# Order of the operand loads, sub-chunk size and engine of small copies at the start of a linear-attention and two-MLP kernel

## The chip, the cores and the metric

One core of a Trainium2 chip runs the whole program. The metric is device time in microseconds (us). Three timed runs of the kernel before gave 1028.97 us (median), 1026.72 us (lowest) and 1031.26 us (highest). The engines are named as the profile names them: PE (matrix products; PEld is its weight load), DVE (vector), ACT (scalar), POOL (GpSimd), SP (the queue that issues most transfers).

## The reference

Three layers in a row, all in float32. The first is a linear attention with a decay and a bonus for the present token, for 4 sequences of 768 tokens, 8 heads of 48 values:

```python
for t in range(S):
    cur = einsum('bhd,bhe->bhde', u[None] * k[t], v[t])
    y[t] = einsum('bhd,bhde->bhe', r[t], state + cur)
    state = w[t][..., None] * state + einsum('bhd,bhe->bhde', k[t], v[t])
x = y.reshape(3072, 384)
x = ((x @ w_a) * (x @ w_b)) @ w_out            # 384 -> 1536 -> 384
h = x @ w_in                                   # 384 -> 2048
out = (max(h, 0) + alpha * min(h, 0)) @ w_out2 # 2048 -> 384
```

## The kernel before, in words

**Units.** The attention is cut into 12 units: 128 tokens of two of the four sequences, all heads. A unit's work is written in `unit(u, pr)` from line 336. It needs its operands twice: transposed (tile `T`, r, k and w of 112 partitions by 1024 values each, 1.376 MB, `ld_t`, line 378) and natural (tile `N`, three parts of 128 by 768 values, 0.393 MB each, `ld_n`, line 382), and its values (`V`, 0.393 MB, `ld_v`, line 395), which also go straight from memory into four places of the tile `Z` (`ld_z`, line 400, four transfers).

**What a unit computes.** `natural(d, p)` (line 440) makes on DVE the terms of tokens that are d apart within a sub-chunk of C tokens, C from the list `SUBS` (4 for unit 0, 8 for unit 1): a product into `e`, a sum over it (line 486), and an update of k. The result `A` is written to memory (`mb`, line 511) and read back by eight transfers of 16 KB to the diagonal blocks of `M` (`place`, line 517). Beyond C, `level(h, bs, p)` (line 545) makes the terms of two neighbouring strips of h tokens on PE (`psl`, line 567), and `extract` copies them to `M` on ACT (line 585; for unit 1 half of them on DVE, line 583). Between the levels `tree(h, p)` (line 520) scales r and k in place on DVE (a 112x1024 product and a short one for each of six h). Then r is copied to `M` (`rcopy`, line 597), k is transposed (`ktrans`), `dstate` and `state` carry the state, and `yout` (line 698) makes the rows of y for the products in `psx`, which ACT and DVE split into a high and a low part (`x`).

**Blocks.** Two units make a block of 512 tokens. `mlp1` (line 781) runs the first MLP of a block in 12 steps: 9 products into `pa`, 9 into `pb`, 9 into `acc`, each with a weight tile of its own: 36 weight tiles in all, for all six blocks. `mlp2` (line 902) does the second MLP for six chunks of tokens with 32 more weight tiles.

**Weights.** They come as 64-bit words of 384 KB a tile. `load_w` (line 270) issues the load from POOL (line 290); where a tile lies more than `WL` = 6 behind, POOL first copies one element of the finished tile six before it (`tick`, line 289), which is how the load is held back. The fourth tile waits for a zeroed tile of the first unit (line 286). Then ACT makes three steps over the tile (`sign` L295, `expo` L307, `low` L301), DVE joins them (L310), ACT writes the high part (L316) and DVE the low part. The tile in between, `ws`, has three buffers.

**The order of the work.** `Tasks` (line 35) is a planner in the program itself. Each step has an engine, a duration, an urgency (lower is earlier), and the names it reads and writes. `run()` (line 94) walks the steps through a model of the engines and of one transfer queue (0.33 MB per us and 2.2 us), and emits them in the order of the model; each engine then works strictly in that order. While the first products are not there, `filler()` (line 138) puts products of the 128x128 identity with itself (`warm`, line 988) into PE's order, from 4.5 us of the model on. The loads of units 0 and 1 have urgencies near -260 to -215 (lines 407 to 424): N of unit 0, `un`, the identity, T of unit 0, N of unit 1, T of unit 1; the values of both only after the diagonal blocks of unit 0 (`diags`, line 409). The loads of unit 2 wait for the diagonal blocks of unit 1.

## Time and profile before

| What | Value |
|---|---|
| median of three runs | 1028.97 us |
| profiled execution: span from its first to its last instruction | 1026.6 us |
| PE, PEld busy | 984.9 us, 846.2 us |
| DVE busy | 743.5 us |
| ACT, POOL busy | 419.1 us, 91.3 us |
| mean granted clock of PE | 0.990 |
| first products of the first MLP | at 78.93 us |
| first products of the second MLP | at 614.34 us |

The profiled execution has a span of 1026.6 us; the page gives no other time for it, so the time around the span is taken as what the median of the timed runs has more, 2.4 us. All times within the span count from its first instruction. Busy times of PE overlap a little, since matmuls are pipelined; an engine that is idle matters only where another that sets the end waits for it.

### The profile page before, as it was taken

What the parts mean: (1) busy time and instruction counts of PE and PEld (TensorE: products, weight loads), DVE (VectorE), ACT (ScalarE), POOL (GpSimd) and SP (SyncE); (2) the same over time, 40 slices, a digit from 0 to 9 for tenths busy, and PEclk for the clock granted to TensorE, in tenths of its full rate; (3) what the DMA queues carried; (4) which work ended last, traced back from release to release, by engine and by line L of the source; (5) the groups of instructions that cost most, each with busy time, mean ns of one, the idle gap of its engine ahead of it and who ended that gap; (6) DMA issues with size and microseconds to landing.
All of it is one profiled execution on the core that took longest, in us unless ns stands there. A gap on an engine that the chain in (4) does not pass through costs nothing.

```text
span 1026.6 us, 22621 instructions
## 1 busy us (share of the span) xinstructions
PE 984.9 (96%) x9616; PEld 846.2 (82%) x9616; DVE 743.5 (72%) x1241; ACT 419.1 (41%) x866; POOL 91.3 (9%) x173
## 2 busy tenths in 40 slices
PE   5879989999999999999999999999999999999998
PEld 5778767887788878778888888999998999998988
DVE  7869898979989999898944667455555554555544
ACT  2477988433332353534347994121221211211111
POOL 3033230100100010001003341000000000000000
PEclk9889999999999999999999999999999999999999
DMA  9584573052341434315115551010010100000000
GB/s 273 112 238 138 161 232 111 32 142 61 113 122 22 126 85 106 111 33 171 19 42 185 169 184 63 1 31 31 18 45 1 31 31 1 1 32 1 31 1 31
DMA packets 75092, 85.70 MB, mean 83 GB/s; under 512 B 55216, under 2 KB 64560, under 8 KB 72368
## 3 DMA queue, kind: packets, MB, share of 16 engines
q1 hardware_dynamic: 67824, 52.81, 19.0%
q0 software_dynamic: 7168, 31.46, 9.3%
q8 instruction: 75, 1.23, 0.5%
q14 instruction: 25, 0.20, 0.1%
HBM read 73.24 MB, written 11.01 MB: 82 GB/s over the span
## 4 chain that ended last, share of the span: by engine, by line
PE 61%; DVE 18%; ACT 10%; DMA 5%; issue 4%; SPq 1%; ACTq 0%; DVEq 0%
PE acd L769 20%; PE hp L769 19%; PE pa L769 6%; PE acc L769 5%; PE pb L769 5%; DVE T L257 4%; DVE e L257 4%; DVE A L486 3%; DMA T<-in_rkw_t_dram 2%; PE warm L988 2%; ACT ws L295 2%; PE psl L567 2%; ACT ws L301 2%; DMA n<-in_rkw_n_dram 2%; DVE a L257 2%
## 5 line engine op out<-in xcount | busy, mean ns | idle before, releaser
L769 PE MATMUL acd<-w,g 128*128 128x384 f32 x1152 | 216.5, 336 | 0.0
L769 PE MATMUL hp<-x,w 128*128 128x512 f32 x864 | 214.9, 393 | 0.7 <-DVE g L927 0.7
L769 PEld LDWEIGHTS acd<-w,g 128*128 128x128 f32 x1152 | 203.8, 188 | 7.9
L769 PEld LDWEIGHTS hp<-x,w 128*128 128x128 f32 x864 | 161.0, 188 | 30.9 <-DVE g L927 1.1
L932 ACT CAST g<-g 128x512 fp32r<-128x512 f32 x96 | 59.6, 621 | 299.6 <-PE acd L769 262.2
L257 DVE TENSOR_TENSOR g<-g,g 128x512 fp32r<-128x512 f32 x96 | 66.1, 689 | 152.3 <-ACT g L932 151.9
L769 PE MATMUL acc<-g,w 128*128 128x512 f32 x648 | 174.5, 398 | 0.0
L769 PE MATMUL pa<-x,w 128*128 128x512 f32 x648 | 162.2, 394 | 4.0 <-DVE w L257 1.8
L769 PE MATMUL pb<-x,w 128*128 128x512 f32 x648 | 160.0, 391 | 0.2 <-DVE a L257 0.2
L769 PEld LDWEIGHTS pa<-x,w 128*128 128x128 f32 x648 | 121.4, 189 | 31.3 <-DVE w L257 2.5
L769 PEld LDWEIGHTS pb<-x,w 128*128 128x128 f32 x648 | 121.4, 188 | 26.5 <-DVE a L257 0.8
L769 PEld LDWEIGHTS acc<-g,w 128*128 128x128 f32 x648 | 118.1, 188 | 24.5 <-DVE g L257 0.2
L257 DVE TENSOR_TENSOR T<-T 112x1024 f32<-112x1024 f32 (+3 forms) x144 | 116.0, 808 | 17.2 <-DMA T<-in_rkw_t_dram 13.2
L831 ACT CAST g<-a 128x512 fp32r<-128x512 f32 x72 | 44.5, 618 | 117.0 <-DVE a L257 115.0
L923 DVE TENSOR_SCALAR g<-hp,al 128x512 f32<-128x512 f32 x96 | 72.0, 750 | 21.1 <-PE hp L769 18.4
L486 DVE TENSOR_REDUCE A<-e 128x16 f32<-128x768 f32 (+15 forms) x148 | 85.8, 579 | 1.9
L927 DVE SCALAR_TENSOR_TENSOR g<-hp,g 128x512 f32<-128x512 f32 x96 | 66.3, 690 | 2.9
L820 ACT COPY a<-pa 128x512 f32<-128x512 f32 x72 | 42.0, 583 | 55.2 <-PE pa L769 54.9
L257 DVE TENSOR_TENSOR a<-a,pb 128x512 f32<-128x512 f32 x72 | 49.1, 682 | 17.5 <-PE pb L769 16.1
L567 PEld LDWEIGHTS psl<-T 48*16 48x16 f32 (+3 forms) x3072 | 34.0, 98 | 27.6 <-issue 14.1
L257 DVE TENSOR_TENSOR g<-a,g 128x512 fp32r<-128x512 f32 x72 | 49.4, 686 | 7.4 <-ACT g L831 7.2
L567 PE MATMUL psl<-T 48*16 48x16 f32 (+3 forms) x3072 | 37.4, 183 | 17.6 <-DVE T L257 10.5
(68 smaller groups left out, 885.5 us busy)
## 6 DMA issues: line engine op xcount, KB each, us to landing
raw<-in_wt_dram POOLq DMA_DIRECT2D x68, 384.0 KB, 4.1
T<-in_rkw_t_dram SPq DMA_DIRECT2D x12, 1344.0 KB, 8.5
N<-in_rkw_n_dram SPq DMA_DIRECT2D x10, 1152.0 KB, 6.7
x2d<-x POOLq DMA_DIRECT2D x36, 128.0 KB, 2.1
x2r<-x2d SPq DMA_DIRECT2D x36, 128.0 KB, 2.2
out_dram<-o SPq DMA_DIRECT2D x24, 192.0 KB, 1.9
V<-in_v_s_dram SPq DMA_DIRECT2D x11, 384.0 KB, 5.6
Z<-in_v_s_dram SPq DMA_DIRECT2D x44, 96.0 KB, 3.0
```

The lines of the kernel that those rows point to most:

```text
L257: nc.vector.tensor_tensor(out=out, in0=a, in1=b, op=op)
L295: nc.scalar.activation(out=c["s"].bitcast(F16).rearrange("p (n b) -> p n b", b=2)[:, :, 1], in_=c["raw"][:, :, 1].bitcast(F32), func=ACTF. ...
L301: nc.scalar.activation(out=c["s"].bitcast(U16).rearrange("p (n b) -> p n b", b=2)[:, :, 0], in_=c["raw"][:, :, 0], func=ACTF.Copy, scale=7 ...
L486: nc.vector.tensor_reduce(out=v[:, :, d:d + (n - 1) * (SUB + 1) + 1:SUB + 1], in_=part(st["e"], 0, n), axis=AX.X, op=ALU.add)
L567: nc.tensor.matmul(out=st["ps"][o0:o0 + ms, cc, q, zc * i:zc * i + zc], lhsT=t[b0:b0 + 48, 1, q0 + q, t0:t0 + ms], rhs=r[b0:b0 + 48, q0 + ...
L769: nc.tensor.matmul(out=out, lhsT=lhsT, rhs=rhs, start=start, stop=stop)
L820: nc.scalar.copy(c["a", f], c["pa"])
L831: nc.scalar.copy(c["g", f][:, 0], c["a", f])
L923: nc.vector.tensor_scalar(out=st["m", f], in0=st["h", f], scalar1=0.0, scalar2=al[:, f:f + 1], op0=ALU.min, op1=ALU.mult)
L927: nc.vector.scalar_tensor_tensor(out=st["m", f], in0=st["h", f], scalar=0.0, in1=st["m", f], op0=ALU.max, op1=ALU.add)
L932: nc.scalar.copy(st["g", f][:, 0], st["m", f])
L988: nc.tensor.matmul(out=warm["ps"][:, 0:128], lhsT=idt, rhs=idt, start=True, stop=True)
```

## The change

`SUBS[1]` goes from 8 to 4, so unit 1 has four distances on DVE and one more level (h = 4) on PE. The transposed operands come in three transfers each (k, r, w) and are the first that SP issues, for unit 0; then N of unit 0, T and N of unit 1, the identity, the values. The values no longer wait for the diagonal blocks, nor do the loads of unit 2. The four transfers into `Z` of each unit become four POOL copies from `V`. The first six weight loads wait for the last natural operand of unit 1 (POOL reads one element of it). `expo` moves from ACT to POOL; `ws` has two buffers in place of three; slots of the weight pool may be taken in any order. For units 0 and 1 the state and y are made in two halves of 64 tokens (`dstate` and `yout`), `rcopy` copies only the second half, DVE takes fewer of unit 1's copies from `psl` and one more of `kn`. `warm` multiplies a tile of ones that DVE sets, from 1.5 us of the model on. The urgencies of the first block and of the weights change. The cut-down diff (comments that were dropped, and changes of names only, are left out):

```diff
-SUBS = [4, 8, 4, 8, 16, 16, 16, 16, 16, 16, 16, 16]
+SUBS = [4, 4, 4, 8, 16, 16, 16, 16, 16, 16, 16, 16]
...
-    ANY = ("ws", "psacc")
+    ANY = ("ws", "psacc", "w")
...
+    ones = const.tile([128, 128], F32, name="ones")
...
-    for tag, n in (("w", NW), ("ws", 3), ("x2", 2), ...
+    for tag, n in (("w", NW), ("ws", 2), ("x2", 2), ...
...
-        gate = len(prev) == int(4)
-        if gate:
-            after = list(after) + ["m1/d3"]
+        gate = not prev
+        prev.append(nm)
+        if len(prev) <= WL and nm[1] in "abo":
+            after = list(after) + ["N1in"]
...
-                nc.gpsimd.tensor_copy(tick, first_m[1][0:1, 0, 0, 0:1])
+                nc.gpsimd.tensor_copy(tick, cur["N", 1][2][0:1, 0, 0:1])
...
-            nc.scalar.activation(out=h, in_=h, func=ACTF.Copy, scale=2.0 ** -112)
+            nc.gpsimd.tensor_single_scalar(out=h, in_=h, scalar=2.0 ** -112, op=ALU.mult)
...
-        add("ACT", act(384), pr, expo, r=[raw], w=[raw + "/h"])
+        add("Pool", 1.2, pr, expo, r=[raw + "/h"], w=[raw + "/h"])
...
-        def ld_z():
-            for cc in range(2):
-                for hd in range(2):
-                    nc.sync.dma_start(
-                        out=zv(cc, hd)[64 * hd:64 * hd + 64], in_=v_s[u, 64 * cc:64 * cc + 64, hd])
+        def cp_z(cc, hd):
+            nc.gpsimd.tensor_copy(zv(cc, hd)[64 * hd:64 * hd + 64], cur["V", u][64 * cc:64 * cc + 64, hd])
...
-        p0 = pr(0) - 30 if u > 1 else -220 + 2 * u
+        p0 = pr(0) - 30 if u > 1 else -260 + 4 * u
...
-        after_diag = diags[1] if u == 2 else []
...
+        for i, y in enumerate("krw"):
+            add("SP", 0.45, p0 + i, lambda y=y: ld_t(y), r=[f"{T}/new"], ..., nbytes=112 * 4096)
+        for i, y in enumerate("krw"):
+            add("SP", 0.3, p0 + (1.1 + 0.1 * i if u > 1 else 3 + 0.1 * i), lambda y=y: ld_n(y), ..., nbytes=128 * 3072)
...
-            r = diags[0] if u < 2 else []
-            add("SP", 0.6, p1, ld_v, r=r, w=[V], ...)
-            add("SP", 2.4, p1, ld_z, r=r, ...)
+            add("SP", 0.6, p1, ld_v, w=[V], ...)
+            for cc in range(2):
+                for hd in range(2):
+                    add("Pool", 0.9, p1 + 30, lambda cc=cc, hd=hd: cp_z(cc, hd), r=[V], w=[zn(cc, hd, "V")])
...
-                    if both and hd:
+                    if both and hd and h >= 16:
                         nc.vector.tensor_copy(dst, src)
...
+            if early:
+                dst, src = dst[:, :, 1], src[:, :, 1]
...
+            if early:
+                for i in range(nd):
+                    add("PE", 0.7, p + i, lambda i=i: run((i,)), r=[kn + "/0", kn + "/1", V], ...)
+                return
...
+            if early:
+                add("PE", 0.8, p - 1, lambda: mms((0,)), ..., r=[x for x in mr if not x.endswith("R")] + ...)
+                add("PE", 0.8, p, lambda: mms((1,)), w=[ps], work=1024, r=mr + zr[1])
...
-            natural(d, pr(-0.1))
+            natural(d, pr(-0.1) if not early else pr(0.1))
...
-    K.fill = [lambda: fill(), 0.22, 4.5, 400.0]
+    K.fill = [lambda: fill(), 0.22, 1.5, 400.0]
...
-        nc.tensor.matmul(out=warm["ps"][:, 0:128], lhsT=idt, rhs=idt, start=True, stop=True)
+        nc.tensor.matmul(out=warm["ps"][:, 0:128], lhsT=ones, rhs=ones, start=True, stop=True)
...
-        start = [52]
+        start = [40]
...
-            start.append(start[-1] + max(..., 100 if j == 0 else 0))
+            start.append(start[-1] + max(..., 95 if j == 0 else 0))
...
+                if u < 2:
+                    names += unit(u, lambda x, u=u: -120 + 40 * x + 5 * u)
+                    continue
```

## Rows read from the trace of the kernel before

**Rows 1.** Busy time by stage: window, length, PE, PEld, DVE, ACT, POOL, PEclk, DMA share, GB/s.
```profile
0.00:78.90 78.90, 57.27 (x1416) 54.13 (x1417) 59.36 (x105) 39.97 (x99) 19.67 (x32) 0.89 0.75 208
78.90:185.80 106.90, 98.82 (x1514) 79.43 (x1512) 98.11 (x171) 86.96 (x197) 25.58 (x43) 1.00 0.52 150
185.80:274.00 88.20, 86.01 (x1095) 69.89 (x1094) 80.27 (x142) 33.28 (x61) 3.93 (x8) 1.00 0.33 91
274.00:559.00 285.00, 279.62 (x3311) 228.45 (x3310) 248.17 (x434) 121.18 (x254) 17.55 (x37) 0.99 0.33 91
559.00:623.00 64.00, 63.35 (x280) 52.12 (x279) 42.97 (x78) 62.51 (x133) 21.35 (x51) 1.00 0.49 163
623.00:1026.60 403.60, 399.84 (x2010) 362.20 (x2008) 214.60 (x315) 75.22 (x127) 3.22 (x6) 1.00 0.07 22
```

**Rows 2.** The chain that ended last, its first 80 us: start, us, what.
```profile
4.01 17.46 DMA n<-in_rkw_n_dram
...
30.99 4.85 PE warm L988 x21
...
59.79 2.22 issue
```

**Rows 3.** Busy time by short windows, columns as in Rows 1.
```profile
3.00:4.00 1.00, 0.00 (x0) 0.00 (x0) 0.84 (x2) 0.00 (x0) 1.00 (x1) 1.00 1.04 390
...
24.00:26.00 2.00, 0.00 (x0) 0.00 (x0) 2.00 (x3) 0.00 (x0) 0.00 (x0) 0.89 0.98 228
```

**Rows 4.** Instructions in order of time: DVE, SP, ACT and PE to 186 us.
```profile
30.17 2.36 DVE L257 TENSOR_TENSOR T<-T 112x1024 f32<-112x1024 f32 x2 [1.64 <-DMA T<-in_rkw_t_dram]
...
50.54 0.25 DVE L486 TENSOR_REDUCE A<-e 128x2 f32<-128x96 f32 x1
...
50.81 0.33 SPq L511 DMA_DIRECT2D mb<-A  x1
...
56.16 5.26 SPq L518 DMA_DIRECT2D M<-mb  x8
...
66.77 0.82 ACT L585 COPY M<-psl 8x128 f32<-8x128 f32 x4
...
78.93 2.32 PE L769 MATMUL pa<-x,w 128*128 128x512 f32 x9
...
185.80 2.20 PE L769 MATMUL pa<-x,w 128*128 128x512 f32 x9
```

**Rows 5.** Groups of DVE and ACT, 0 to 78.9 us: xcount | busy us, mean ns | idle before, releaser.
```profile
L257 DVE TENSOR_TENSOR T<-T 112x1024 f32<-112x1024 f32 x13 | 15.8, 1223 | 8.4 <-DMA T<-in_rkw_t_dram 4.9 <-PE psl L567 3.5
...
L257 DVE TENSOR_TENSOR e<-n,n 128x480 f32<-128x480 f32 x1 | 0.7, 653 | 0.0
...
L316 ACT CAST w<-ws 128x384 fp32r<-128x384 f32 x10 | 5.0, 503 | 0.0
...
L585 ACT COPY m<-psl 4x64 f32<-4x64 f32 x4 | 0.8, 204 | 11.4 <-DMA m<-mb 11.3
```

**Rows 6.** Groups of ACT and POOL, 78.9 to 185.8 us, columns as in Rows 5.
```profile
L307 ACT ACTIVATE raw<-raw 128x384 f32<-128x384 f32 x25 | 14.0, 560 | 0.3
...
L289 POOL COPY tick<-w 1x1 f32<-1x1 f32 x21 | 15.0, 715 | 54.6 <-ACT w L316 54.6
L290 POOL DMA_DIRECT2D raw<-in_wt_dram x21 | 11.3, 538 | 1.9 <-issue 0.7 <-DVE e L257 0.6 <-DVE g L257 0.3
```

**Rows 7.** Instructions of POOL and DVE in order of time, 96 to 101 us.
```profile
96.01 3.44 POOL L289 COPY tick<-w 1x1 f32<-1x1 f32 x1 [12.09 <-ACT w L316]
99.93 0.17 POOL L289 COPY tick<-w 1x1 f32<-1x1 f32 x1
...
97.13 1.22 DVE L257 TENSOR_TENSOR T<-T 112x1024 f32<-112x1024 f32 x1
99.33 0.68 DVE L257 TENSOR_TENSOR a<-a,pb 128x512 f32<-128x512 f32 x1
```

**Rows 8.** POOL's groups over the whole span: a zeroing of 2048 values a partition.
```profile
L977 POOL MEMSET Z<- 128x2048 f32 x1 | 1.8, 1805 | 0.3 <-POOLq L1133 0.3
```

More of the change, by code (lines that the diff above doesn't have):

```diff
@@ L354, in bank @@
         def bank(lev):
-            if u < len(BLOCKS[0]) and lev:
+            if early and u:
                 return "acc", "psacc"
@@ L553, in level @@
             tag, pool = bank(True)
-            nf = NF[h] if u < len(BLOCKS[0]) and K.fill else 0
             def mms():
@@ L617, in cp @@
                     cur["kn", u] = new_kn().rearrange("p (q d) -> p q d", d=112)
-                nc.scalar.copy(cur["kn", u][:, 4 * g:4 * g + 4], st[g])
+                if both and g:
+                    nc.vector.tensor_copy(cur["kn", u][:, 4 * g:4 * g + 4], st[g])
+                else:
+                    nc.scalar.copy(cur["kn", u][:, 4 * g:4 * g + 4], st[g])
             add("PE", 0.4, p, tr, r=[f"{T}/k.{g}", "idt"], w=[ps], alloc=(pool, ps), work=392)
-            add("ACT", act(448, True), p, cp, r=[ps], w=[f"{kn}/{g}"], alloc=("kn", kn) if g == 0 else None)
+            add("DVE" if both and g else "ACT", act(448, True), p, cp, r=[ps], w=[f"{kn}/{g}"], alloc=("kn", kn) if g == 0 else None)
         def dstate(p):
@@ L626, in dstate, with run @@
             tag, pool = bank(False)
-            def run():
+            def run(ccs=tuple(range(nd))):
                 k, v = cur["kn", u], cur["V", u]
-                pss = [pp.tile([128, 8, D], F32, tag=tag, name=f"psd{i}", bufs=3) for i in range(nd)]
-                cur["ds", u] = pss
+                pss = cur.setdefault(("ds", u), {})
+                for i in ccs:
+                    pss[i] = pp.tile([128, 8, D], F32, tag=tag, name=f"psd{i}", bufs=3)
                 for q in range(8):
                     for hd in range(2):
-                        for cc in range(nd):
+                        for cc in ccs:
                             hh = hd ^ cc
@@ L998, in rwkv_then_moe_kernel @@
             add("HOST", 0, -310, lambda: None, w=[n + "/x"], alloc=("w", n))
-        add("DVE", 0.5, -201, lambda: zeros(nc.vector, [cur["A", 0]] + A16), w=["A16", "A0/x"])
-        add("DVE", 1.0, -200, lambda: zeros(nc.vector, St), w=[f"St{i}.{b}" for i in range(2) for b in range(2)])
+        add("Pool", 0.5, -205, lambda: zeros(nc.gpsimd, [cur["A", 0]]), w=["A0/x"])
+        add("DVE", 0.1, -400, lambda: nc.vector.memset(ones, 1.0), w=["ones"])
+        add("DVE", 0.3, -199, lambda: zeros(nc.vector, A16), w=["A16"])
+        add("DVE", 1.0, -199, lambda: zeros(nc.vector, St), w=[f"St{i}.{b}" for i in range(2) for b in range(2)])
         def first():
@@ L1053, in weights @@
                     next(gens[i - n], None)
-        weights((load_w((nm, f), wt1[f, i], start[0] + (start[1] - start[0]) / F1 * f - wlead + i)
-                 for f in range(F1) for i, nm in enumerate("abo")), WL - 1)
+        d = (start[1] - start[0]) / F1
+        w1 = [("a", f, 0) if i == 0 else ("b", f, 1) if i == 1 else ("o", f, 2) for f in range(F1) for i in range(3)]
+        weights((load_w(f"w{nm}{f}", wt1[f, i], start[0] + d * (f + 0.3 * i) - wlead - (25 if f < 2 else 0))
+                 for nm, f, i in w1), WL - 1)
         for j in range(NB):
@@ L1068, in rwkv_then_moe_kernel @@
         s2 = start[NB]
-        w2 = [("ip"[i], f) for f in range(F2) for i in range(2)]
-        weights((load_w((nm, f), wt2[f, "ip".index(nm)], start[NB - 1] + 4 + 1.8 * i, ["p2"])
-                 for i, (nm, f) in enumerate(w2)), min(4, WL - 1))
+        weights((load_w(f"w{'ip'[i]}{f}", wt2[f, i], start[NB - 1] + 4 + 3.6 * f + 1.8 * i, ["p2"])
+                 for f in range(F2) for i in range(2)), WL - 1)
         d = 63.0
```

155 lines of the change are left out of this document (73 added, 82 removed).

## The prediction

> **What bounds the kernel now.** I read the busy time by stage first. From 78.9 us on PE is busy 98.82 of 106.90, 86.01 of 88.20, 279.62 of 285.00, 63.35 of 64.00 and 399.84 of 403.60 us [rows 1]: 927.6 of 947.7. The reader is to see that behind the first product of the first MLP PE sets the end nearly alone; 20 us of idle time are all that a better order can win there, and 8.1 of them lie in block 0 (78.9 to 185.8 us). DVE has 98.11 us of work in the 106.90 of block 0 and is 89% busy from 185.8 to 559 us (328.5 of 373.2) [rows 1]: it follows PE closely, so an earlier PE is of use only where DVE comes along.
>
> So the question is why the first product starts at 78.93 us [rows 4]. In the chain of waits its head is a transfer, N of unit 1, for 17.46 us; then PE's filler products and short stops called "issue" [rows 2]. In order of time, DVE's first product on T of unit 1 waits until 30.17 us, the last sum of unit 1's natural terms starts at 50.54, `mb` is issued at 50.81, its way back into M takes SP from 56.16 to 61.42, ACT's copies that need it begin at 66.77, and the product follows at 78.93 [rows 4]. From `mb` to the product are 28.1 us. PE was not short of time there: much of its 57 us of work is filler.
>
> **The loads.** Before the operands of unit 1 six weight tiles of 0.393 MB went out, 2.36 MB in all, and T of unit 1 was the last. Alone on the queues T moved at 228 GB/s; N moved at 390 [rows 3]. Now T of unit 0 comes first, then N, then T and N of unit 1. With a start of the flow at 2.4 us (an estimate, from the busy window at 3 us in rows 3): 1.376 / 0.228 = 6.0, so T at 8.4; 1.18 / 0.39 = 3.0, so N at 11.4; T of unit 1 at 17.4 and its N at 20.4 us. All 5.11 MB at the one or the other rate bound the last landing at 15.5 and 24.8. SP issues six transfers for T in place of two and is past all of its loads in under 10 us; the values, now ahead of the diagonal blocks on SP, are 0.8 MB behind N. The weights pay: POOL stands at its first tick until N of unit 1 is there, and behind it stand six weight loads and eight copies into Z, for which `sign` on ACT and `yout` wait. They land between about 22 and 29 us; the first product needs two of them by 50 or so, so this wait is hidden; without that cover it costs what R2 prices.
>
> **DVE up to `mb`.** Eight distances are 9696 values a partition in products, sums and updates; four are 5184. At 653 ns for 480 [rows 5] a value costs 1.36 ns: 13.2 against 7.1 us, 6 us saved. From 8.4 us DVE has the natural terms of unit 0 (7.1) and three levels of its tree (1.22 [rows 5] and about 0.5 for the short part, 5.2), which is 20.7 us, when N of unit 1 is there; then unit 1's terms (7.1) and two levels (3.4): `mb` goes out at about 31 us in place of 50.8. Nothing on DVE before 8.4 us is missed.
>
> **From `mb` to the first product.** The 28.1 us [rows 4] are the way out and back and the copies behind it. The new level costs ACT 16 copies of 0.204 us [rows 5], 3.3 us, and ACT takes over what DVE copied of h = 8, about 1 us. Eight transfers into Z fall away on SP, `rcopy` is halved, state and y come in halves, and half of a `kn` copy goes to DVE: some 3 us. The write of `mb` no longer meets the weights, which are in by 29 us. Less queueing at ACT (the ACT copies began 5.3 us behind SP's last issue) may give 3 us more, and the rest of unit 0's tree, seven products of 1.22 us, still has to run on DVE beside it. I take 25 us, from 20 to 31. The first product then starts at 31 + 25 = 56 us, 23 earlier, with ends of 46 and 66.
>
> **Block 0.** `expo` leaves ACT: 25 tiles of 0.560 us, 14.0 us of the 86.96 that ACT works there [rows 1, 6]. But 10 tiles were finished before the first product [rows 5]; with loads from 22 us on and the two units packed I count about 5. So five more tiles fall into block 0, 5.5 us for DVE, and its 98.1 us become 103.6.
> A POOL operation of 384 values has no row. Between a zeroing of 2048 in 1805 ns [rows 8], scaled to 0.34 us, and the 0.560 us that ACT took for the step, I take 0.34, as the zeroing ran on POOL itself. What it costs DVE: the one-element copy at 96.01 lasted 3.44 us, to 99.45, while DVE ran products of two operands in SBUF, and ended just behind the start of one (99.33) that takes its second operand from PSUM; the copy at 99.93 took 0.17 [rows 7]. So POOL's reads wait for such gaps, and what DVE loses lies between nothing and the whole of 0.56 for each of 31 `expo` and 8 copies into Z: 0 to 22 us. I take half of 0.34 each, 7 us, nearer to nothing because in the row it is POOL that waits. DVE then has 110.6 us; some 2 us of it can slip, as the last part of block 0 holds terms of unit 4. Block 0 goes from 106.9 to 109 us, +2; ends: 98.8 (all idle time of PE gone) and 129.
> The Trainium skill (SBUF — State Buffer, "Who interferes with whom") states that a DVE instruction with two SBUF inputs and a GpSimd instruction that reads SBUF exclude each other for the whole instruction, and that whichever is issued first blocks the other. The trace agrees for POOL (3.44 against 0.17 us); that DVE is held as well no row here shows, and by the rule the 7 us would be 13 at 0.34 each.
>
> **Later.** 32 copies into Z fall into blocks 1 to 4, 0 to 18 us for DVE by the same bounds, beside 44.7 us of idle time of DVE [rows 1]; I take 2 us, 0 to 8. In the second MLP `expo` costs nothing: from 559 to 623 us ACT is busy 62.51 of 64 us, yet PE 63.35 [rows 1], so PE's products cover it; were they gone, 32 tiles of 0.34 us on POOL would show. Two `ws` buffers instead of three are covered as long as a tile leaves them fast (R2). The tile of ones lets filler run 4 us sooner, on no chain.
>
> **The sum** on the profiled execution: 1026.6 - 23 + 2 + 2 = 1007.6 us. The median of the runs lies 2.4 above the span: 1010 us, or 19 below 1028.97. Since PE's own work behind the first product stays, the gain at the start should reach the end.
>
> **Rivals.** *R1, POOL's queue holds the weights.* For each tile POOL has a tick of 0.715, an issue of 0.538 [rows 6] and now `expo` of 0.34 plus a wait like the tick's (0.715 - 0.17 = 0.55): 2.14 us; 31 tiles are 66 us, within block 0. If its two reads wait 1.4 us each it is 3.9 us a tile, block 0 becomes 121 us, and the time 1010 + 12 = 1022. For it: the 3.44 us [rows 7], and POOL is strictly in order, so `expo` stands behind ticks that wait for ACT. Against: the mean tick. *R2, slower: two buffers of `ws` with a step on POOL between.* A tile is now held through ACT, POOL, ACT, DVE, ACT and DVE. If only two tiles are ready at the first product, 34 go through two buffers; at 8 us each they need 136 us. Block 0 grows by 27 over my 109 and the time is 1037. It decides from 7.8 us a tile on. For it: DVE and ACT are both near full in block 0 [rows 1]; against: the bare work of a tile is about 4 us, and planned urgencies put tiles ahead. The same mechanism with the weights later still only lengthens it. *R3, more is won.* The first product at 50, the idle time of PE in block 0 gone (-8.1) and nothing lost later: 1026.6 - 29 - 8 + 2.4 = 992. For it: ACT loses 14 us of work just where its steps fill the stretch. *R4, the change does not do what it says:* PE's order is that of the planner's model, filler included; if that order keeps PE as late as now, the time is about 1027 to 1029. Against it: filler is put in only where the model has nothing else.
>
> **How the numbers follow.** Forecast 0.55, with a range of its own of 1002 to 1019; R1 0.16, R2 0.12, R3 0.13, R4 0.04. About 0.5% (5 us) is what a measurement of this kernel can tell from no change, so faster means below 1023.8. Faster: 0.55 + 0.13 + 0.07 of R1 = 0.75; same: 0.09 of R1 + 0.04 = 0.13; slower: 0.12. The range of 994 to 1030 leaves out R2 and a part of R3; its ends come from a first product at 46 with block 0 as before or shorter, and from block 0 at 129 us.
>
> **What would show it.** The first product (`pa`) near 56 us; T of unit 1 on DVE by about 18 us; `mb` of unit 1 at about 31; the first product of block 1 near 56 + 109 = 165 us in place of 185.80 [rows 4]; PE's idle time behind it no larger than now. Wrong it would be if `pa` starts late because ACT or SP, not DVE, holds unit 1; if block 0 lasts over 120 us with waits of `pa`, `pb` on weights (R1: POOL waits for DVE; R2: `sign` waits for a `ws`); or if DVE's two-operand products become longer beside POOL and later blocks wait for `x`.

## The result, and the profile after

The changed kernel takes 1042.65 us (median of four runs, 1042.48 to 1044.37), the kernel before 1027.85 us on the same chip (1024.07 to 1031.26). The ratio is 1.0148, 95% interval 1.0119 to 1.0176: 1.5% slower, outside the predicted range of 994 to 1030 us, where a time of 1010 us had been forecast. The profiled execution has a span of 1040.9 us against 1026.6.

Busy time by stage of the kernel after, cut where the first product of a block (`pa`) starts; columns as in [rows 1]:

```profile
0.00:78.40 78.40, 66.86 (x1625) 63.84 (x1626) 60.43 (x97) 28.21 (x91) 28.14 (x34) 0.93 0.62 186
78.40:193.30 114.90, 99.90 (x1487) 78.63 (x1486) 98.57 (x160) 83.54 (x183) 82.23 (x97) 0.93 0.46 139
193.30:282.40 89.10, 88.09 (x1106) 72.31 (x1105) 81.72 (x143) 33.12 (x61) 10.14 (x14) 1.00 0.29 83
282.40:559.60 277.20, 269.59 (x3262) 220.02 (x3261) 241.23 (x422) 111.06 (x234) 29.93 (x42) 0.99 0.25 73
559.60:631.00 71.40, 71.40 (x317) 59.12 (x316) 42.21 (x73) 51.26 (x97) 49.70 (x82) 1.00 0.53 167
631.00:1040.90 409.90, 406.45 (x2038) 367.35 (x2036) 225.70 (x335) 88.80 (x153) 17.62 (x23) 1.00 0.08 27
```

Before it can be compared, a bound of [rows 1] has to be put right. PE's timeline of the kernel before shows three starts of nine `pa` products there; a block has 108 of them, and the 109th is the one at 179.00. So 185.80 us is step 1 of block 1, not its start:

```profile
172.86 2.22 PE L769 MATMUL pa<-x,w 128*128 128x512 f32 x9
...
179.00 2.20 PE L769 MATMUL pa<-x,w 128*128 128x512 f32 x9
...
185.80 2.20 PE L769 MATMUL pa<-x,w 128*128 128x512 f32 x9
```

The busy time of the kernel before, block 0 between its true bounds:

```profile
78.90:179.00 100.10, 92.02 (x1484) 73.80 (x1482) 91.31 (x161) 85.16 (x193) 25.30 (x42) 1.00 0.55 160
```

The reader is to see three things. The first product comes at 78.4 us where it came at 78.9: the start won nothing. Block 0 takes 114.9 in place of 100.1 us, with PE idle for 15.0 in place of 8.1 us and busy for 7.9 us longer at a mean granted clock of 0.93 in place of 1.00. And from block 1's first product to the end it is 847.6 us in both kernels: blocks 1 to 5 take 2.4 us longer in the kernel after, and the second MLP 2.4 us less. So on balance the whole loss, 14.3 us of span, arises in block 0.

What PE waited for in block 0 of the kernel after:

```profile
PE acc L777 <- ACT g L839: 4.5, 3, 3.4
PE psl L557 <- DVE T L258: 4.5, 2, 3.2
PE psx L714 <- issue: 3.7, 1, 3.7
PE pa L777 <- DVE w L258: 1.3, 1, 1.3
```

Each line gives the us in total, the times and the longest. PE waits for a finished tile (`w`) for only 1.5 us (0.2 of it in a smaller group); it waits for ACT and DVE, which also prepare the tiles, and once for "issue", a stop for which the profile names no cause (more on these under No. 10). The three long waits (3.2, 3.7 and 3.4 us, ending at 91.6, 125.5 and 185.4 us) are 10.3 of the 15.0 us of idle time, and during or right behind each of them the granted clock fell to 0.50, the lower of its two levels, 1.2 GHz (90.3 to 97.1, 124.4 to 131.3 and 185.9 to 189.3 us). The 7.9 us of longer busy time go with these three spells: in block 0 the kernel before had no wait over 2.1 us and a clock of 1.00.

The start of the kernel after in order of time (timelines of DVE, SP, ACT, POOL and PE, put together; start, duration, and idle time before with its releaser):

```profile
8.74 1.23 DVE L258 TENSOR_TENSOR T<-T 112x1024 f32<-112x1024 f32 x1 [2.34 <-DMA T<-in_rkw_t_dram]
20.82 1.62 POOL L293 COPY tick<-n 1x1 f32<-1x1 f32 x1 [16.29 <-DMA n<-in_rkw_n_dram]
30.87 1.23 DVE L258 TENSOR_TENSOR T<-T 112x1024 f32<-112x1024 f32 x1 [3.09 <-PE psl L557]
43.52 0.34 SPq L504 DMA_DIRECT2D mb<-A  x1
47.14 1.11 ACT L323 CAST w<-ws 128x384 fp32r<-128x384 f32 x2 [15.88 <-DVE ws L317]
48.15 6.05 ACT L575 COPY m<-psl 4x64 f32<-4x64 f32 x29
54.11 3.90 ACT L575 COPY M<-psl 4x64 f32<-4x64 f32 x24
60.65 0.96 DVE L258 TENSOR_TENSOR e<-N,un 128x768 f32<-128x768 f32 x1 [4.74 <-DMA N<-in_rkw_n_dram]
67.31 1.12 ACT L302 ACTIVATE ws<-raw 128x384 f16<-128x384 f32 x2
```

The transfers land as predicted (8.74 and 20.82 us), and `mb` of unit 1 goes out 7.3 us sooner than before (43.52 against 50.81, [rows 4]), though not at 31. But the 28.1 us from `mb` to the first product became 34.9, and the start was level again. ACT made the first steps over two tiles by 31.3 us and then stood 15.88 us at the first `hi`, as DVE came to the `join` in front of it only at 46.55 us, behind the terms of unit 1. The copies of both units followed, and ACT began the next tile (`sign`) at 67.31 us.

**All kernels, read in the same way.** "Ready" counts weight tiles whose `hi` began before the first product; "36th" is the start of the last `hi` of the first MLP's tiles; then the first products of block 1 and of the second MLP. "Median" is that of the timed runs, in us. The other times come from one profiled execution of each kernel. That of No. 14 is the slowest of its 12 runs (1033.31 us) and that of No. 15 the fastest of its 9 (1021.64 us), so 2 or 3 us between two rows can be chance. The ratio is to the kernel before, timed on the same chip, where its median was 1027.85 us for the kernel after and 1029.72 to 1031.45 for the others; a forecast in us is to be read with that in mind.

| No. | Kernel | 1st product | Ready | 36th | Block 1 | MLP 2 | Median | Ratio to before, 95% |
|---|---|---|---|---|---|---|---|---|
| | before | 78.9 | 10 | 175.1 | 179.0 | 614.3 | 1027.85 | 1 |
| | after | 78.4 | 4 | 191.9 | 193.3 | 631.0 | 1042.65 | 1.0148 [1.0119, 1.0176] |
| 1 | after, no `expo` | 87.5 | 5 | 183.3 | 183.9 | 626.4 | 1039.56 | 1.0077 [1.0052, 1.0101] |
| 2 | after, `expo` on ACT | 86.9 | 4 | 195.8 | 196.2 | 633.3 | 1049.44 | 1.0173 [1.0143, 1.0204] |
| 3 | after, three `ws` | 79.5 | 6 | 181.5 | 183.4 | 626.2 | 1040.46 | 1.0082 [1.0056, 1.0108] |
| 4 | after, Z by transfer | 86.5 | 6 | 189.9 | 191.6 | 630.7 | 1044.87 | 1.0124 [1.0090, 1.0157] |
| 5 | after, 30 tiles | 79.8 | 4 | 173.0 (30th) | 179.0 | 629.7 | 1041.81 | 1.0097 [1.0060, 1.0134] |
| 6 | after, no filler | 73.7 | 4 | 185.8 | 187.1 | 625.4 | 1036.94 | 1.0058 [1.0034, 1.0081] |
| 7 | after, unit 2 held back | 77.7 | 4 | 189.9 | 192.2 | 631.5 | 1043.24 | 1.0105 [1.0064, 1.0146] |
| 8 | after, natural first | 81.9 | 5 | 187.3 | 189.6 | 629.6 | 1039.71 | 1.0082 [1.0055, 1.0109] |
| 9 | before, no filler | 75.0 | 9 | 174.4 | 177.2 | 613.7 | 1027.39 | 0.9978 [0.9960, 0.9995] |
| 10 | before, sub-chunks of 4 | 88.2 | 7 | 179.2 | 191.1 | 624.0 | 1039.34 | 1.0106 [1.0071, 1.0141] |
| 11 | after, weights not held | 86.1 | 6 | 189.3 | 189.5 | 627.6 | 1040.18 | 1.0109 [1.0082, 1.0137] |
| 12 | after, three `ws`, no filler | 74.2 | 4 | 176.8 | 181.7 | 625.3 | 1036.94 | 1.0074 [1.0048, 1.0099] |
| 13 | after, sub-chunks of 8 | 87.7 | 7 | 189.8 | 191.0 | 630.8 | 1042.05 | 1.0115 [1.0088, 1.0141] |
| 14 | before, weights held | 80.1 | 10 | 179.4 | 185.0 | 619.3 | 1030.74 | 1.0001 [0.9981, 1.0021] |
| 15 | before, weights held, no filler | 72.5 | 9 | 172.2 | 176.3 | 607.7 | 1022.47 | 0.9946 [0.9922, 0.9969] |
| 16 | after, path of a tile as before | 80.4 | 5 | 180.1 | 183.1 | 629.7 | 1039.95 | 1.0089 [1.0058, 1.0121] |
| 17 | before, path of a tile as after | 79.0 | 8 | 186.6 | 188.4 | 624.5 | 1039.55 | 1.0094 [1.0058, 1.0130] |
| 18 | after, weights' steps late, no filler | 74.9 | 2 | 190.7 | 189.2 | 627.9 | 1040.01 | 1.0086 [1.0052, 1.0120] |

Two limits of block 0 can be read from the table. Block 1 starts 0 to 6 us behind the 36th tile in all kernels but No. 10 (11.9 us) and No. 18 (its product came 1.5 us ahead). And it starts 96 us or more behind the first product: 96.4 to 109.3 us where that comes at 86 us or later (Nos. 1, 2, 4, 10, 11 and 13), 114.9 in the kernel after. The first of these is an order in time and shows no cause yet; Nos. 5, 16 and 17 try it.

### The profile page after: what moved, and what is told of

Read it like the earlier page. It is cut to its first block, busy times and chain, and to the rows that moved or that the text cites. A ratio compares the mean times of both kernels' runs of the same rounds, so it can differ in the third digit from the quotient of the medians.

```text
span 1040.9 us, 23170 instructions
## 1 busy us (share of the span) xinstructions
PE 1002.3 (96%) x9826; PEld 861.3 (83%) x9826; DVE 749.9 (72%) x1226; ACT 396.0 (38%) x817; POOL 217.8 (21%) x290
## 4 chain that ended last, share of the span: by engine, by line
PE 66%; DVE 21%; issue 4%; DMA 3%; ACT 3%; POOL 2%; SPq 1%; DVEq 0%; POOLq 0%; ACTq 0%
PE acd L777 19%; PE hp L777 19%; PE acc L777 7%; PE pa L777 7%; PE pb L777 6%; DVE T L258 5%; DVE e L258 4%; DVE A L479 3%; PE warm L995 3%; DMA T<-in_rkw_t_dram 2%; DVE a L258 2%; PE psl L557 2%; DVE N L258 2%; DVE g L258 2%; DMA N<-in_rkw_n_dram 2%
## 5 line engine op out<-in xcount | busy, mean ns | idle before, releaser
L777 PE MATMUL acc<-g,w 128*128 128x512 f32 x648 | 177.8, 404 | 4.5 <-ACT g L839 4.5
L940 ACT CAST g<-g 128x512 fp32r<-128x512 f32 x96 | 59.6, 621 | 295.8 <-PE acd L777 255.2
L777 PE MATMUL pb<-x,w 128*128 128x512 f32 x648 | 163.0, 396 | 0.8 <-DVE a L258 0.5
L777 PEld LDWEIGHTS acc<-g,w 128*128 128x128 f32 x648 | 122.0, 193 | 31.0 <-ACT g L839 5.3
L258 DVE TENSOR_TENSOR T<-T 112x1024 f32<-112x1024 f32 (+4 forms) x144 | 121.9, 846 | 24.5 <-DMA T<-in_rkw_t_dram 16.2
L314 POOL TENSOR_SCALAR raw<-raw 128x384 f32<-128x384 f32 x68 | 90.6, 1339 | 82.6 <-ACT ws L302 79.7
L404 POOL COPY Z<-V 64x384 f32<-64x384 f32 x40 | 35.6, 891 | 246.5 <-PE psx L714 238.5
L479 DVE TENSOR_REDUCE A<-e 128x8 f32<-128x384 f32 (+15 forms) x144 | 83.5, 580 | 2.0
L935 DVE SCALAR_TENSOR_TENSOR g<-hp,g 128x512 f32<-128x512 f32 x96 | 66.3, 690 | 2.9
L258 DVE TENSOR_TENSOR g<-a,g 128x512 fp32r<-128x512 f32 x72 | 50.1, 696 | 16.8 <-ACT g L839 16.4
```

What stands on the lines that cost most here:

```text
L258: nc.vector.tensor_tensor(out=out, in0=a, in1=b, op=op)
L314: nc.gpsimd.tensor_single_scalar(out=h, in_=h, scalar=2.0 ** -112, op=ALU.mult)
L404: nc.gpsimd.tensor_copy(zv(cc, hd)[64 * hd:64 * hd + 64], cur["V", u][64 * cc:64 * cc + 64, hd])
L479: nc.vector.tensor_reduce(out=v[:, :, d:d + (n - 1) * (SUB + 1) + 1:SUB + 1], in_=part(st["e"], 0, n), axis=AX.X, op=ALU.add)
L777: nc.tensor.matmul(out=out, lhsT=lhsT, rhs=rhs, start=start, stop=stop)
L935: nc.vector.scalar_tensor_tensor(out=st["m", f], in0=st["h", f], scalar=0.0, in1=st["m", f], op0=ALU.max, op1=ALU.add)
```

## The experiments

The theories at the start: **T**, too few tiles are ready at the first product and block 0 runs at the pace at which tiles are finished; **P**, POOL's `expo` sets that pace; **B**, the two `ws` buffers do; **D**, POOL's copies hold DVE. Later came **F** (filler stands in PE's way), **G** (the loads of unit 2 hold unit 1's transfers), **L** (the order of T and N), **S** (the sub-chunks), **W** (P and B together, the path of a tile), **U** (the packing of the first two units), **H** and **I** (what holds the first product).

**1 and 2: `expo` left out (and `join` shifts the word right), or back on ACT.** The diff of the second:

```diff
-            nc.gpsimd.tensor_single_scalar(out=h, in_=h, scalar=2.0 ** -112, op=ALU.mult)
+            nc.scalar.activation(out=h, in_=h, func=ACTF.Copy, scale=2.0 ** -112)
```

> The changed kernel without the step expo on POOL (the exponents of the weights are left unscaled and shifted the other way when joined, so the products work on tiny numbers; all else as it is). Theory T (too few tiles ready: block 0 ends with the 36th weight tile, and the changed kernel enters it with 4 finished tiles in place of 10; the pace of some 3.5 us a tile is the same in both kernels and comes from ACT, DVE and the hand-overs): the step itself is a small part, time 1036 to 1043 us, block 0 lasts 108 to 115 us. Rival P (expo on POOL, in order and behind DVE's reads, sets the pace): 1026 to 1033 us, block 0 about 100 us. Rival D (POOL's reads hold DVE): 3 to 6 us less, with shorter DVE products.

> The changed kernel with expo back on ACT. T: ACT has 0.56 us more a tile, so the pace gets no better: 1042 to 1050 us. P: as without expo or nearly, 1028 to 1035 us.

Without the step the 36th tile comes 8.6 us sooner and the ratio falls from 1.0148 to 1.0077. On ACT it comes 3.9 us later and nothing is won. The time is in T's range; the length of block 0, 96.4 us, is nearer to P's, but the first product also came 9.1 us later. So the step costs some 7 us where it stands, but ACT with two buffers has no better place for it: POOL as such is not the whole cause.

**3: three buffers.**

```diff
-            c["s"] = xp.tile([128, 384], U32, tag="ws", name="ws", bufs=2)
+            c["s"] = xp.tile([128, 384], U32, tag="ws", name="ws", bufs=3)
```

> The changed kernel with three buffers of ws in place of two. T: one more tile can be finished before the first product and the hand-overs overlap a little more: 1036 to 1041 us. Rival B (two buffers set the pace): 1027 to 1033 us, block 0 about 100 us. P: no change, 1041 to 1044 us.

The 36th tile comes 10.4 us and block 1 9.9 us sooner, the second MLP only 4.8: the third buffer matters in block 0, and half of it is lost again behind. The time, 1040.46 us, is T's and not B's.

**4: the values into Z by SP's transfers, as before.**

> The changed kernel with the values of all units placed into Z by four transfers from memory on SP, as before, in place of POOL copies from V. T: 1040 to 1044 us, block 0 as long as in the changed kernel. D (POOL's copies hold DVE or the queue of the weights): 1035 to 1039 us.

1.0124 against 1.0148, with intervals that overlap: D is not borne out.

**5: block 0 with six tiles fewer** (steps 2 and 3 use the tiles of steps 0 and 1).

> The changed kernel in which steps 2 and 3 of the first MLP use the weight tiles of steps 0 and 1 (six tiles of 36 are left out, loads and preparation; the result of the first MLP is that of other weights). It gives the first products six tiles more of a lead, as many as the kernel before had. Theory T (block 0 is paced by the preparation of tiles, about 3.5 us each, and ends with the last of them): block 0 loses 14 to 20 us of its 115, block 1 starts near 178 us, time 1023 to 1030 us. Rival (block 0 is simply full of DVE work): 6 tiles of 1.1 us on DVE, 1034 to 1038 us.

Block 1 starts at 179.0 us, where T expected it, with the first product 1.4 us later: T holds for block 0. Yet the second MLP starts only 1.3 us sooner, and the time, 1041.81 us, lies above both forecasts. PE's waits from block 1's start to the second MLP:

```profile
PE psx L714 <- DMA M<-mb: 11.6, 5, 3.8
```

In the kernel after there is no such wait in that stretch. The units now hold the blocks, and what block 0 gives is lost again.

**6: no filler on PE.**

```diff
-    K.fill = [lambda: fill(), 0.22, 1.5, 400.0]
+    K.fill = [lambda: fill(), 0.22, 1.5, 1.6]
```

> The changed kernel without the filler products on PE. Theory F (filler in PE's fixed order holds the first units back, as DVE's products on T wait for PE): the first product at 65 to 73 us in place of 78, and the time 5 to 10 us shorter unless the clock of PE falls. Rival (DVE's and ACT's own order, and the way of the diagonal blocks, hold the first product): first product at 76 us or later, time 1040 to 1047 us, with a lower clock before it.

The first product comes 4.7 us sooner and the ratio falls to 1.0058, the lowest of any single edit on the changed kernel (the intervals of Nos. 1, 3 and 8 overlap with it). `mb` of unit 1 goes out at 37.61 us in place of 43.52. F holds in part.

**7 and 8: the loads of unit 2 wait for unit 1's diagonal blocks; natural operands ahead of the transposed ones.**

> The changed kernel with the loads of unit 2 waiting for the diagonal blocks of unit 1 again. Theory G (terms of units 2 and 3 stand on DVE ahead of the last steps of units 0 and 1 and wait there for their loads): the first product at 69 to 74 us; T then says that fewer tiles are ready and that work moves into block 0, so the time gains less, 1038 to 1043 us. Rival: first product at 77 us or later.

> The changed kernel with the natural operands ahead of the transposed ones for units 0 and 1. Theory L (with T first, the sums of unit 0 and so its diagonal blocks come later, and the copies behind them hold PSUM and ACT): first product at 72 to 76 us, time 1036 to 1040 us. Rival (the order of the loads is without effect on the start): first product at 78 to 82 us, time 1041 to 1046 us.

G falls: the first product moves by 0.7 us. With the natural operands first it comes 3.5 us later, and the time is yet better (1.0082 against 1.0148, intervals apart): the first product's time alone does not set the end.

**9 and 10: on the kernel before, no filler, or sub-chunks of 4 in unit 1.**

```diff
-SUBS = [4, 8, 4, 8, 16, 16, 16, 16, 16, 16, 16, 16]
+SUBS = [4, 4, 4, 8, 16, 16, 16, 16, 16, 16, 16, 16]
```

> The kernel before without filler products on PE. If filler stands in the way of unit 1's short products (theory F, -4.7 us to the first product in the changed kernel), the first product comes at 72 to 76 us in place of 78.9. If tiles of weights set block 0 (theory T: block 1 starts within 4 us of the 36th tile, about 3.5 us each), that tile moves by less than the first product does: 36th tile at 171 to 175, block 1 at 175 to 178 in place of 179.0, and the time is 1024 to 1029 us. Rival: the filler does what it is for; without it the granted clock falls in the first 100 us, block 0 grows, and the time is 1032 to 1040.

> The kernel before with unit 1 in sub-chunks of 4 and nothing else. By the prediction's step on DVE (6 us of natural terms saved up to mb, a tree level more behind it, net 4 to 6 us) the first product comes at 73 to 76 us and the time falls to 1023 to 1027. By the theory that the written-out orders of PE, ACT and DVE with their waits on each other set the first product (it did not move in the changed kernel though T and N came as predicted), it stays at 77 to 82. By theory T the time then follows the count of tiles ready: 9 to 10 ready, block 1 at 177 to 182, time 1026 to 1033.

Without filler the kernel before gains 0.2%, its first product 3.9 us, both as F and T expected. The sub-chunks alone, which the prediction counted as a gain of 6 us, move the first product 9.3 us later and the time up by 1.06%, against all three forecasts. `mb` of unit 1 does go out 13.9 us sooner (36.91 against 50.81 us), but from there to the first product it takes 51.3 us in place of 28.1. PE's timeline of that kernel shows 7.15 us of it in one place, a stop in the middle of one group of products:

```profile
56.38 1.21 PE L567 MATMUL psl<-T 48*16 48x16 f32 x126
64.73 0.21 PE L567 MATMUL psl<-T 48*16 48x16 f32 x2 [7.15 <-issue]
```

"issue" means that PE waited for no semaphore that the profile shows. The transfers during this stop (57.59 to 64.73 us; packets, MB, share of the 16 DMA engines):

```profile
q1 hardware_dynamic: 129, 1.23, 67.8%
q0 software_dynamic: 97, 0.51, 27.7%
q8 instruction: 1, 0.02, 1.1%
```

The first two are operands and weights and fill the DMA engines. The third is one transfer of 16 KB of instructions, from 61.87 to 63.18 us, and PE goes on 1.55 us behind its end. The other stops of this sort fit: of 105 stops of PE of over 1 us put down to "issue" in the twenty traces, 96 end 1.2 to 1.7 us behind the end of such a transfer, though one comes only every 13 us or so (77 in 1036 us here); by chance it would be about 4. So in these stops PE in all likelihood waited for its own next instructions. Whose instructions a transfer holds the trace does not say, that the other transfers held this one up is not shown, and no run took the stops away.

**11: the first six tiles not held behind the operands. 12: three buffers and no filler.**

```diff
-        gate = not prev
+        gate = False
...
-            after = list(after) + ["N1in"]
+            after = list(after)
```

> The changed kernel with its first six weight tiles not held back behind the operands: they go out from the start, as POOL can. Theory T: ACT and DVE work on tiles while the operands come, so 7 to 9 tiles are ready at the first product in place of 4; the operands land some 6 us later and the first product at 80 to 86; block 0 takes 98 to 105 us in place of 114.9, block 1 starts at 182 to 188 and the time is 1032 to 1039. Rival: tiles were few because ACT and DVE had no room for them beside the units, not because weights came late: still 4 to 5 ready, block 1 at 195 or later, 1044 us or more.

> The changed kernel without filler and with three buffers of ws: two gains found one by one (-6 us each at block 1's start from 193.3, or less where both free the same wait). If they add: first product at 74 to 76, block 1 at 177 to 181, time 1027 to 1033 (the early blocks gave back some 6 us later with three buffers, where products of the units waited for M). If both only moved the same 36th tile: block 1 at 182 to 186 and 1034 to 1038.

No. 11: the first product came at 86.1 us as expected of later operands, but only 6 tiles were ready, of which two came after 78 us: weights that come at once do not make tiles ready. No. 12: block 1 starts at 181.7 us, 11.6 us sooner than in the kernel after, where the gains of Nos. 3 and 6 add up to 16.1, and the time is no better than without filler alone (1.0074 and 1.0058): lost again in blocks 1 to 5.

**13: sub-chunks of 8 in the changed kernel. 14 and 15: the weights held behind N of unit 1 in the kernel before, with and without filler.**

```diff
-        gate = len(prev) == int(4)
+        gate = len(prev) == 1
...
-            after = list(after) + ["m1/d3"]
+            after = list(after) + ["N1w/x"]
...
-                nc.gpsimd.tensor_copy(tick, first_m[1][0:1, 0, 0, 0:1])
+                nc.gpsimd.tensor_copy(tick, cur["N", 1][2][0:1, 0, 0:1])
```

> The changed kernel with unit 1 back in sub-chunks of 8, all else as changed: the counterpart of the kernel before with sub-chunks of 4 alone, whose first product came at 88.2 us in place of 78.9 and whose time rose by 1.06%. Theory S (the added tree level with its diagonal blocks is what costs): first product at 69 to 75 us in place of 78.4, block 1 at 183 to 187 in place of 193.3, time 1032 to 1037. Theory T alone (only the tiles that are ready count, 4 of 36): wherever the first product lies, the 36th tile stays within 2 us of 191.9, block 1 at 191 to 195, time 1040 to 1044.

> The kernel before with its weights held back behind N of unit 1, and nothing else: the prediction's first step alone. By the prediction's steps T and N of unit 1 land some 7 us sooner (T at about 23 in place of 30 us), mb goes out at 43 to 45 in place of 50.8, the first product comes at 71 to 74, and the time is 1021 to 1025. By theory T fewer tiles are ready (5 to 8 in place of 10), the 36th comes at 174 to 180 in place of 175.1, block 1 at 177 to 183 in place of 179.0, and the time is 1027 to 1034 though the first product comes sooner.

> The same without filler on PE. Without filler the kernel before gained 3.9 us at the first product and 2 us in time. If the two add: first product at 67 to 71 us. By theory T the time follows the 36th tile, 172 to 178 us, block 1 at 175 to 181 and 1024 to 1031; by the prediction's steps 1018 to 1023.

No. 13: S falls as the cause of the loss. The first product comes 9.3 us later, not sooner; block 1 and the time are as T alone expected. An edit of one part changes the order of all (the planner writes it anew), and the part's cost on one kernel is not its cost on the other. No. 14: the order of the loads alone does nothing to the time. The operands of unit 1 no longer make DVE wait, yet `mb` goes out at 50.76 us as before (50.81), as DVE now waits 7.09 us for one level product of PE. 10 tiles are ready as before, so in this kernel weights that come late do not make tiles few. No. 15 is the version that **beats both kernels**: 1022.47 us, 0.54% below the kernel before and some 2% below the changed one. `mb` goes out at 46.47 us and the first product comes at 72.5; the lead over the kernel before is 6.4 us there, 2.7 at block 1 and 6.6 at the second MLP. Its stages:

```profile
0.00:72.50 72.50, 27.18 (x1170) 24.13 (x1170) 57.77 (x103) 38.19 (x96) 18.79 (x31) 0.91 0.81 216
72.50:176.30 103.80, 94.60 (x1480) 75.18 (x1481) 93.18 (x163) 86.56 (x196) 24.32 (x42) 0.98 0.59 162
```

PE is busy for 27.18 us ahead of the first product, against 57.27 us [rows 1], and still the first product comes sooner.

**16 and 17: the path of a tile** (`expo` and the buffers) put back in the changed kernel, and changed alone in the kernel before. The second in short:

```diff
-            nc.scalar.activation(out=h, in_=h, func=ACTF.Copy, scale=2.0 ** -112)
+            nc.gpsimd.tensor_single_scalar(out=h, in_=h, scalar=2.0 ** -112, op=ALU.mult)
...
-            c["s"] = xp.tile([128, 384], U32, tag="ws", name="ws", bufs=3)
+            c["s"] = xp.tile([128, 384], U32, tag="ws", name="ws", bufs=2)
```

> The changed kernel with the whole path of a weight tile as before: expo on ACT and three buffers of ws; the order of the loads, the sub-chunks, state and y by chunk, and the values by POOL stay changed. Theory W (the tile's path sets how many tiles are ready and how fast the rest follow): 7 to 10 ready at the first product in place of 4, 36th tile at 174 to 181 us in place of 191.9, block 1 at 177 to 184, time 1030 to 1036. Rival U (the two first units packed ahead of the weights leave DVE and ACT no room): still 3 to 5 ready, 36th tile at 183 or later, time 1037 or more.

> The kernel before with the changed path of a weight tile alone: two buffers of ws and expo on POOL; the loads, the sub-chunks and the units stay as before. Theory W: 5 to 8 tiles ready, 36th tile at 184 to 192 us in place of 175.1, block 1 at 187 to 194 in place of 179.0, time 1036 to 1045: most of the change's loss by itself. Rival U: 9 to 10 ready, 36th tile at 180 or sooner, time 1028 to 1034.

No. 17 answers W: with the loads, the units and the first product (79.0 us) as before, the 36th tile comes 11.5 us and block 1 9.4 us later, and the time rises by 0.94%. That is two thirds of the loss in block 0. POOL's groups in block 0 of that kernel (busy us, mean ns | idle before), and the waits on a tile's path (us in total, times, longest):

```profile
L307 POOL TENSOR_SCALAR raw<-raw 128x384 f32<-128x384 f32 x27 | 39.7, 1474 | 30.4 <-ACT ws L295 29.7 <-ACT wl L749 0.4
...
L289 POOL COPY tick<-w 1x1 f32<-1x1 f32 x22 | 8.6, 392 | 14.8 <-ACT w L316 14.8
```

```profile
DVE ws L310 <- POOL raw L307: 3.2, 7, 1.1
ACT ws L295 <- DVE w L257: 9.1, 9, 1.9
ACT w L316 <- DVE ws L310: 5.3, 7, 1.4
```

The last two in block 0 of the kernel before:

```profile
ACT w L316 <- DVE ws L310: 2.0, 2, 1.4
ACT ws L295 <- DVE w L257: 1.0, 3, 0.4
```

POOL is not short of time (60.3 us of work in 109.4). It is ACT that stands: 9.1 us at `sign` until DVE's last step frees a `ws`, and 5.3 us at `hi` for DVE's `join`, 14.4 us in all against 3.0 before. What stands behind it in ACT's fixed order waits too.

No. 16 gives the other half of the answer. Block 1 starts at 183.1 us, 10.2 sooner, as W says; but 5 tiles are ready, as U says, and the time is only 0.6% better. PE's waits from block 1 to the second MLP there, and the first of those in the kernel after:

```profile
PE psl L557 <- DVE T L258: 6.7, 5, 2.1
PE psx L714 <- DMA M<-mb: 4.8, 3, 3.7
PE psl L557 <- issue: 2.5, 1, 2.5
```

```profile
PE psl L557 <- DVE T L258: 7.7, 7, 2.1
```

Of the 10.2 us 8.9 are lost in this stretch (446.6 against 437.7 us). PE's idle time grows by 7.1 us there, and the waits for M and the stop account for that.

Nos. 16 and 17 together split the change into the path of a tile and the rest. Block 0 lasts 100.1 us in the kernel before, 109.4 with the path alone (No. 17), 102.7 with all but the path (No. 16) and 114.9 with both. So the path costs 9.3 to 12.2 us there, the rest 2.6 to 5.5. At `sign` and `hi` ACT stands 16.4 us in block 0 of the kernel after and 3.1 in No. 16. In the time of the kernel the path costs 0.6 to 0.9% and the rest 0.5 to 0.9%: with the path undone the loss lies behind block 0, where blocks 1 to 5 take 446.6 us against 435.3 in the kernel before. What in the rest costs that no run shows.

**18: the weights' first steps ordered behind the diagonal blocks, without filler.**

> The changed kernel without filler and with the steps of the first six weight tiles ordered behind the diagonal blocks of unit 1, so that ACT does not stand at a weight's hi (11.8 us of idle time, to 43.2 us) ahead of the copies into m, which began at 44.2. Theory H (that wait at ACT holds the units: PE waited 5.0 us for those copies): the copies begin at 37 to 41 us and the first product comes at 66 to 70 us in place of 73.7; only 0 to 2 tiles are ready then, the 36th comes at 186 to 192 us and the time is 1037 to 1043. Rival I (PE's own stops between the short products, 10.5 us of them before 41 us, hold DVE and with it everything): first product still at 72 to 76.

H is not borne out: ACT's copies begin at 33.7 us, then stop for the diagonal blocks of unit 0 until 41.5, and the first product comes at 74.9 us. As most of the copies start only 2.7 us sooner than in No. 6, this tries H weakly. PE's waits up to 79 us:

```profile
PE psl L558 <- DVE T L258: 17.5, 4, 13.9
PE psl L558 <- issue: 14.6, 5, 4.8
```

This is what rival I expects, and each of the five stops ends 1.1 to 1.6 us behind a transfer of instructions, as under No. 10. But no run took PE's stops away, so I is not shown.

## Why the prediction was wrong, point by point

- **The loads: right.** T at 8.74 and N of unit 1 at 20.82 us, for 8.4 and 20.4.
- **`mb` at 31 us: wrong by 12.5.** The step added DVE's own work as if it ran without a stop and alone. From 8.7 to 43.5 us DVE was busy for 27.5 us, 4.9 more than the 22.6 counted, with the later products of both trees that stand between the terms in its fixed order, and idle for 7.3, of which 7.2 on PE's level products. PE came to those late through filler and "issue" stops of 2.22, 1.38 and 2.56 us. Without filler (No. 6) `mb` went out at 37.61 us, so filler accounts for 5.9 of the 12.5.
- **25 us from `mb` to the product: wrong by 9.9.** It took 34.9. The step counted ACT and SP and left out the order across units: DVE takes the first term of unit 3 ahead of unit 1's last tree product and waits 4.74 us for its N. That is half of the 9.9; where the rest went is not traced.
- **The first product at 56 us: wrong by 22.4.** The two points above add up to it (12.5 and 9.9), and it is the largest of the terms that failed. It takes away the gain; it does not make the loss.
- **Block 0, +2 us: it grew by 14.8.** This is the step behind the sign. It saw that some 5 tiles would be ready in place of 10 and priced each missing one at 1.1 us of DVE, as work beside other work. No. 5 shows the price in the changed kernel: six tiles fewer move block 1 by 14.3 us, 2.4 us each. But it is not the count alone: with the path of a tile as before (No. 16) block 0 is only 2.6 us longer than before, though 5 tiles are ready. The term that failed most is that path. The sum held the two `ws` buffers to be covered and gave `expo` 0.34 us on POOL; Nos. 16 and 17 show 9.3 to 12.2 us for both together, as ACT stands at `sign` and `hi`. In PE's terms the loss is 6.9 us more of idle time and 7.9 us more of busy time at a lower granted clock. One of its three long waits is an "issue" stop of 3.7 us, and no run shows what block 0 takes without it and without the fall of the clock.
- **Block 0's length before: misread.** It was taken as 106.9 us; it is 100.1, as the bound was a step too far. 109 us then looked like nearly no change. Two smaller slips change nothing: 328.5 of 373.2 us is 88%, not 89, and the ends of 46 and 66 us for the first product do not follow from 31 and 20 to 31, which give 51 and 62.
- **`expo` at 0.34 us: wrong.** It takes 1.34 us in the mean. What DVE loses beside POOL (7 us taken in block 0) is hardly seen in two of its groups: its products on T of 1024 values take 1319 in place of the 1218 ns of the kernel before, 13 of them, and `ws` 595 in place of 551 ns, 32 of them: 2.7 us. By the rule of the Trainium skill (SBUF — State Buffer, "Who interferes with whom") DVE is held as well. These rows agree in sign, with 2.7 us where the prediction drew 13 from the rule.
- **Rivals.** R1 and R2 named the mechanism that No. 17 shows (POOL's step, and two buffers held across it), with 0.28 between them; R2's 1037 us is the nearest of all to 1042.65. They should have been one rival, with the 4 ready tiles in it. That the figure lies so near is in part luck: R2 took two ready tiles and 8 us each, where 4 were ready and a tile held its `ws` for 6.7 us (from the start of `sign` to the end of DVE's low part, mean of 31 in block 0). R4 (PE as late as before) came true for the first product, at a chance of 0.04, but only its time: filler is one part of it (4.7 us in No. 6).

Why does the changed kernel have 4 or 5 tiles ready even with the path undone? Neither the order of the loads (No. 14) nor the sub-chunks (No. 13, 7 ready, but at 87.7 us) explains it. The traces show where the tiles are missing. In the kernel before ACT begins a tile at 50.0, 54.3, 57.8, 59.6 and 66.3 us, in between the copies of the units. In the kernel after it begins none between 30.1 and 67.3 us, in No. 16 none between 49.0 and 75.0; in No. 11, where the first tile is there at 11.7 us, it stands 31.48 us at the first `hi` for DVE's `join`. So the written-out orders of ACT and DVE put the units ahead of the tiles, as U has it. Which part of the change makes them do so stays open: the urgencies of the first two units, state and y by chunk, and other PSUM buffers for these units (`bank`, which the description of the change leaves out) were not tried alone.

## What to carry to other kernels

Ask of each block what must arrive last, and count how many of those are ready when it starts and what one costs from end to end, not on one engine: here block 1 started 0 to 6 us behind the 36th weight tile in 18 of the 20 kernels, wherever the first product lay, and the path of such a tile made most of the loss in block 0. In a kernel whose engines follow written-out orders, a chain of dependent steps over three engines is not the sum of one engine's work; take its length from the same chain in the trace, scaled, and expect each edit to reorder the rest. A cause found by one edit is to be tried on both kernels: put back in the changed one, and put alone into the one before. A buffer taken away and a step moved to an idle engine lengthen the same path, so price them together.

## What was not expected of the hardware

**POOL's step.** In the kernel after, by form, over the whole span:

```profile
L314 POOL TENSOR_SCALAR raw<-raw 128x384 f32<-128x384 f32 x68 | 90.6, 1339 | 82.6 <-ACT ws L302 79.7 <-issue 1.2
...
L404 POOL COPY Z<-V 64x384 f32<-64x384 f32 x40 | 35.6, 891 | 246.5 <-PE psx L714 238.5 <-DMA V<-in_v_s_dram 6.3
```

The same 384 values took ACT 560 ns [rows 6]. POOL's fastest of 68 took 1196 ns, and in block 5, where DVE is busy for 42 of 71 us, the median is 1212: it is the step itself, not waiting beside DVE.

**Filler.** It did what it is for. In No. 6 the trace has no record of the clock before 67.1 us, and a stretch without a record counts as 1.00 in a row of windows (the 0.91 of No. 15 counts its first 52.4 us so). But the products show the level. PE's 112x112 products into `psk`, up to 67 us in No. 6, in the kernel after, and in the kernel before from 63.1 to 66.5 us, with that window's row:

```profile
L607 PE MATMUL psk<-idt,T 112*128 112x112 f32 x16 | 3.6, 399 | 5.3 <-DVE T L258 2.7 <-ACT M L575 2.6
L607 PE MATMUL psk<-idt,T 112*128 112x112 f32 x16 | 1.9, 261 | 1.0 <-DVE T L258 1.0
L613 PE MATMUL psk<-idt,T 112*128 112x112 f32 x8 | 1.8, 401 | 0.0
63.10:66.50 3.40, 3.40 (x25) 3.23 (x19) 1.15 (x3) 2.67 (x7) 0.90 (x2) 0.50 1.10 305
```

At a granted clock of 0.50 (1.2 GHz) one takes 401 ns; 399 ns in No. 6 is that level, 261 in the kernel after is not. With filler, 46.2 us of PE's work up to 79 us, the mean granted clock there was 0.93. And still the first product comes sooner without it in each pair (Nos. 6, 9, 12, 15), and the time falls in three of the four: with three `ws` buffers in the changed kernel (Nos. 3 and 12) it does not. So what the clock gave back here was less than what filler cost; its place in PE's fixed order ahead of short products that DVE waits for is the likely reason.

**PE's stops called "issue".** They go with transfers of instructions (under No. 10): up to 79 us those of over 1 us come to 6.2 us in the kernel after and 13.2 us in No. 6. The prediction saw such stops in [rows 2], but its sum has no term for them.
